# Four attention batches and two feed-forward layers on one core: part of the second layer's weights is rebuilt as float32 during attention

## The chip, the core and the metric

The kernel runs on one core of a Trainium2 chip. The metric is device microseconds of one execution. Engines are called PE (TensorE, with PEld for its weight loads), DVE (VectorE), ACT (ScalarE), POOL (GpSimd) and SP (SyncE, whose queue issues every DMA here).

## The reference, cut to what is computed

Causal attention with a forget gate over 4 batches, 8 heads, 576 positions of 64; its output, 2304 tokens of 512, goes through a first layer (512 to 1024, softmax gate, layer norm, back to 512) and a second (512 to 2048, square of Relu, back to 512).

```python
scores = scale * np.matmul(q, k.transpose(0, 1, 3, 2))
cum = np.cumsum(np.log(np.clip(f, 0.0001, 1.0)), axis=-1)
scores = np.where(causal, -1e9, scores + cum[:, :, :, None] - cum[:, :, None, :])
attn = np.exp(scores - np.max(scores, axis=-1, keepdims=True))
x = np.matmul(attn / (np.sum(attn, axis=-1, keepdims=True) + 1e-09), v)   # then tokens x 512
h = x @ w_in                                                              # 512 -> 1024
solu = h * softmax(h)
ln = (solu - mean(solu)) / np.sqrt(var(solu) + 1e-06) * g_ln
x = ln @ w_out                                                            # 1024 -> 512
h = np.maximum(x @ w2_in, 0.0)                                            # 512 -> 2048
out = h * h @ w2_out                                                      # 2048 -> 512
```

The weights w_in, w_out, w2_in and w2_out arrive as 64-bit floats, everything else as float32.

## The kernel before

**Split products.** A float32 matrix product is made of three products of a faster 32-bit type (fp32r): each operand is split into a rounded high part and the remainder, and high x low, low x high and high x high are added up in PSUM.

**Weights.** Each 64-bit weight is rebuilt as float32 in SBUF from its two 32-bit words by `convert` (L623): a DMA brings the words of 256 columns (256 KB) into a raw buffer (L629), ACT takes the high word (L643), one of ACT, DVE and POOL scales the low word down (through the helper `copy`, L303 to L311), DVE shifts (L647) and puts the sign in (L651), POOL adds the low word (L657). Then `copy` rounds the result to the high part and POOL or DVE subtracts to get the low part (L661). The first layer's weights are converted during the first 115 us (`weights1`). The second layer's weights are cut into 16 blocks of 128 hidden columns, four pieces each, 64 conversions (`weights2`). Their high and low parts go where attention and the first layer leave room: in order, the key buffers K1 and K2, spare ends of these, the first layer's weights and its small buffers. Six raw buffers (the transposed weights `pt`, `adj`, `x` of attention) are used in turn.

**Attention.** 20 tiles of up to 128 queries, 8 heads each. `load_k` and `load_q` bring a tile's keys and queries, in two halves of 4 heads (j = 0, 1); the host has laid out each half twice, on partitions 0 to 63 and 64 to 127, so that high and low part can be made in place. `prep_k` and `prep_q` split them (L421, L456); `picks` (L405) writes constant rows that pick each head's gate sums. For each head: PE makes scores in PSUM (L488), DVE adds the mask and takes the minimum of the negated scores (L509), ACT the exponent (L523), PE transposes (L543), ACT or DVE copies (L303) and, for two heads at a time, PE multiplies by the values (L564). At the end of a tile of tokens, `first` (L786 to L788 and a chain over DVE, ACT and POOL) and `out1` (L727 to L729) apply the first layer; `out1` stores the result split into `x2d` in DRAM.

**Second layer.** Six blocks of 384 tokens, 16 steps each (`step`, L1043). A step is an up product (12 matmuls, L1059 to L1061), Relu (L1067) and square (L1069) on ACT, rounding (L1070) and remainder (L1073) on DVE, and a down product (9 matmuls, L1089 to L1091). Blocks 0 and 1 are run side by side while the weights are converted; blocks 2 to 5 follow with all weights in place.

**Order.** Every operation is a step of a plan. `Plan.lay` (L97) is a list scheduler: it keeps a table of assumed times, takes for every engine the step that can start first (a lower priority number wins a tie), and emits instructions in that order. It may choose among ACT, DVE and POOL for copies and subtractions. Engines and SP's queue then run in that fixed order, each waiting where an operand is not there.

Of the kernel before, what the change touches and what calls it, by code (L numbers as in the profile page):

```python
# [11 lines left out]
U32 = mybir.dt.uint32  # L12
# [15 lines left out]
class Plan:  # L28
# [14 lines left out]
        dma=dict(pe=1000, dve=950, act=910, pool=950, dma=1290),  # L43
# [53 lines left out]
    def lay(self, slack=60):  # L97
# [52 lines left out]
        while todo:  # L150
            pick = None
            for e in engs:
# [23 lines left out]
                if e != "pe":  # L176
# [37 lines left out]
def tile_kernel(ctx: ExitStack, tc: tile.TileContext, q, k, v, f, w_in, w_out, g_ln, w2_in, w2_out, out):  # L214
# [29 lines left out]
    x2d = dram.tile([2, P, KC, NT], F32, name="x2d")  # L244
    sb = ctx.enter_context(tc.tile_pool(name="sb", bufs=1))
# [22 lines left out]
    QN = [new(f"qn{i}", [DM]) for i in range(2)]  # L268
# [116 lines left out]

    def load_q(n, prio):
        load("qn", QN, q, n, prio + 1)

    def load_v(n, prio):
# [7 lines left out]
        pl.add(dict(dma=800), fn, max(prio + 4, V0), writes=[("vn", n % NV)])  # L397

    def picks(i, j):
# [7 lines left out]
        s = pl.add(dict(dve=602, pool=1252) if i else dict(dve=602), fn, -6.9e6 if i == 0 else 5000, ["ident"], [("qa", i, j)], port=True)  # L407

    def prep_k(n, prio):
# [5 lines left out]
        for j in range(2):  # L415
# [7 lines left out]
            def auxrows(y, j=j):  # L423
# [9 lines left out]
                dict(dve=67 + 1.045 * HH * m, pool=119 + 2.213 * HH * m), lo, prio + 2 * j, [("kn", j)] + hk, lk,  # L433
# [9 lines left out]
    def prep_q(n, prio):  # L443
        m = tiles[n]["m"]
        i = n % 2
        for j in range(2):
            q1, q2 = Q1[i][j], Q2[i][j]
            raw = QN[j][:, 0 : HH * m].rearrange("p (h s) -> p h s", s=m)
            for rows, dst, nm in ((LO, q2, "qh"), (HI, q1, "qd")):
                copy(  # L450
                    HH * m, lambda rows=rows, dst=dst: dst[rows, :, 0:m], lambda rows=rows, raw=raw: raw[rows],
                    prio + 2 * j, [("qn", j)], [(nm, i, j)], (), SC, False,
                )

            def lo(q1=q1, q2=q2, raw=raw):
                nc.vector.scalar_tensor_tensor(  # L456
                    out=q1[LO, :, 0:m], in0=raw[LO], scalar=SC, in1=q2[LO, :, 0:m].bitcast(F32), op0=ALU.mult,
# [883 lines left out]
```

## Time and profile before

| | us |
|---|---|
| median of 3 runs | 898.15 |
| lowest, highest | 897.89, 899.88 |
| the profiled execution's own time | 895.01 |
| its span, first to last instruction | 892.9 |

The profile is of one execution. Its page gives for the whole span: PE busy 841.4 us (94%), PEld 728.5 (82%), DVE 459.4 (51%), ACT 496.5 (56%), POOL 294.1 (33%). These are averages over parts that differ; a table of busy times by stretch tells the parts apart. "Idle before" names how long an engine stood before an instruction and the engine and line that released it. The granted clock is TensorE's, 1.00 being 2.4 GHz.

### The profile page before, as it was taken

What the parts mean: (1) busy time and instruction counts of PE and PEld (TensorE: products, weight loads), DVE (VectorE), ACT (ScalarE), POOL (GpSimd) and SP (SyncE); (2) the same over time, 40 slices, a digit from 0 to 9 for tenths busy, and PEclk for the clock granted to TensorE, in tenths of its full rate; (3) what the DMA queues carried; (4) which work ended last, traced back from release to release, by engine and by line L of the source; (5) the groups of instructions that cost most, each with busy time, mean ns of one, the idle gap of its engine ahead of it and who ended that gap; (6) DMA issues with size and microseconds to landing.
All of it is one profiled execution on the core that took longest, in us unless ns stands there. A gap on an engine that the chain in (4) does not pass through costs nothing.

```text
span 892.9 us, 15185 instructions
## 1 busy us (share of the span) xinstructions
PE 841.4 (94%) x5360; PEld 728.5 (82%) x5360; DVE 459.4 (51%) x1139; ACT 496.5 (56%) x1286; POOL 294.1 (33%) x379
## 2 busy tenths in 40 slices
PE   3788899999999999999996999999999999999998
PEld 2556777888888888888875988899999999999997
DVE  6878666655655556655676789722222222222221
ACT  6889878666866667756675777523322222222222
POOL 6567756223521236211387788700000000000000
PEclk9979999999999999999998999999999999999999
DMA  6723335222511125010544644105002002000000
GB/s 219 233 86 126 106 108 157 83 59 66 171 48 37 59 67 165 29 42 24 162 145 132 223 140 131 48 1 177 36 0 72 36 1 71 36 1 1 36 0 36
DMA packets 55499, 75.26 MB, mean 84 GB/s; under 512 B 7456, under 2 KB 35104, under 8 KB 55424
## 3 DMA queue, kind: packets, MB, share of 16 engines
q1 hardware_dynamic: 55424, 74.30, 26.6%
q8 instruction: 42, 0.69, 0.3%
q14 instruction: 33, 0.27, 0.1%
HBM read 59.91 MB, written 14.30 MB: 83 GB/s over the span
## 4 chain that ended last, share of the span: by engine, by line
PE 77%; DVE 9%; DMA 5%; ACT 5%; issue 3%; POOL 2%; SPq 0%; POOLq 0%; DVEq 0%; ACTq 0%
PE pp L1059 6%; PE pp L1061 6%; PE pp L1060 6%; PE z L488 6%; PE pp L543 6%; PE xo L564 6%; PE pp L727 3%; PE hp L786 3%; PE hp L787 3%; PE hp L788 3%; PE pp L728 3%; PE pp L729 3%; PE hp L1089 2%; PE hp L1090 2%; PE hp L1091 2%
## 5 line engine op out<-in xcount | busy, mean ns | idle before, releaser
L1067 ACT ACTIVATE q<-pp 128x384 f32<-128x384 f32 x96 | 47.1, 491 | 223.1 <-PE pp L1061 221.0
L1070 DVE CAST q<-q 128x384 fp32r<-128x384 f32 x96 | 42.1, 438 | 243.4 <-PE xo L1091 92.3
L523 ACT ACTIVATE adj<-z,st 64x288 f32<-64x288 f32 (+9 forms) x192 | 94.9, 497 | 31.0 <-DVE st L509 29.3
L488 PE MATMUL z<-k,q 128*128 128x256 f32 (+17 forms) x384 | 95.1, 347 | 12.7 <-DVE q L456 9.1
L509 DVE CUSTOM_DVE_ANT_0 z<-z,maskb 128x128 f32<-128x128 f32 (+8 forms) x144 | 65.6, 464 | 52.8 <-PE z L488 49.9
L303 ACT COPY pt<-pp 128x384 f32<-128x384 f32 (+5 forms) x170 | 67.9, 420 | 39.0 <-PE pp L543 37.3
L543 PE MATMUL pp<-ident,adj 128*128 128x128 f32 (+1 forms) x480 | 78.7, 280 | 8.7 <-ACT adj L523 8.4
L727 PE MATMUL pp<-ln,woh 128*128 128x256 f32 x288 | 84.2, 292 | 2.3 <-ACT pt L303 2.3
L728 PE MATMUL pp<-ln,wol 128*128 128x256 f32 x288 | 80.8, 280 | 0.0
L729 PE MATMUL pp<-ln,woh 128*128 128x256 f32 x288 | 80.7, 280 | 0.0
L543 PEld LDWEIGHTS pp<-ident,adj 128*128 128x128 f32 (+1 forms) x480 | 52.8, 143 | 30.2 <-ACT adj L523 19.4
L488 PEld LDWEIGHTS z<-k,q 128*128 128x128 f32 (+3 forms) x384 | 58.4, 188 | 19.7 <-ACT q L305 7.9
L564 PE MATMUL xo<-pt,vn 128*64 128x128 f32 (+1 forms) x960 | 70.3, 278 | 3.8 <-ACT pt L303 3.1
L564 PEld LDWEIGHTS xo<-pt,vn 128*64 128x64 f32 x960 | 50.6, 140 | 23.6 <-issue 11.8
L786 PE MATMUL hp<-wih,xl 128*128 128x512 f32 x144 | 61.5, 427 | 2.2 <-ACT hp L825 1.8
L727 PEld LDWEIGHTS pp<-ln,woh 128*128 128x128 f32 x288 | 55.1, 191 | 5.3 <-ACT pt L303 2.6
L787 PE MATMUL hp<-wil,xh 128*128 128x512 f32 x144 | 57.2, 397 | 0.5 <-POOL wil L661 0.5
L788 PE MATMUL hp<-wih,xh 128*128 128x512 f32 x144 | 57.2, 397 | 0.0
L728 PEld LDWEIGHTS pp<-ln,wol 128*128 128x128 f32 x288 | 55.0, 191 | 0.5
L729 PEld LDWEIGHTS pp<-ln,woh 128*128 128x128 f32 x288 | 54.8, 190 | 0.0
L1069 ACT ACTIVATE q<-q 128x384 f32<-128x384 f32 x96 | 50.4, 525 | 2.5
L307 POOL TENSOR_SCALAR q<-qn 64x512 fp32r<-64x512 f32 (+1 forms) x43 | 28.0, 652 | 55.3 <-PE z L488 50.0
(470 smaller groups left out, 2233.5 us busy)
## 6 DMA issues: line engine op xcount, KB each, us to landing
x2d<-xc SPq DMA_DIRECT2D x72, 128.0 KB
kn<-in_k_dram SPq DMA_DIRECT2D x32, 256.0 KB
qn<-in_q_dram SPq DMA_DIRECT2D x32, 256.0 KB
vn<-in_v_dram SPq DMA_DIRECT2D x20, 256.0 KB
ln<-x2d SPq DMA_DIRECT2D x24, 192.0 KB
out_dram<-pt SPq DMA_DIRECT2D x18, 256.0 KB
pt<-in_moe_w_in_dram SPq DMA_DIRECT2D x17, 256.0 KB
ln<-in_moe_w_in_dram SPq DMA_DIRECT2D x8, 512.0 KB
```

The costliest lines, as they stand in the source:

```text
L303: nc.scalar.copy(dst(), src())
L488: nc.tensor.matmul(dst, lhsT=ql[0:r, p, 0:m], rhs=rhs, start=(g == 0), stop=(g == 1))
L509: nc.vector.tensor_tensor_reduce(out=z, in0=z, in1=maskb[0:m, o : o + e - a], scale=1.0, scalar=st[0:m, 0:1] if y else 3e38, op0=ALU.add, ...
L523: nc.scalar.activation(out=adj[0:m, c[1] : c[2]], in_=Z[c[0]][0:m, 0 : c[2] - c[1]], func=AF.Exp, bias=st[0:m, low : low + 1], scale=-1.0, ...
L543: nc.tensor.transpose(at(sk)[:, (c - g) * m : (c - g + 1) * m], adj[0:m, zc : zc + P], ident[0:m, 0:m])
L564: nc.tensor.matmul(XO[own[j], p, off : off + m], lhsT=VN[vslot[b, c]][:, (2 * p + j) * D : (2 * p + j + 1) * D], rhs=pts[j][:, c * m : (c ...
L727: nc.tensor.matmul(px, lhsT=woh[:, fc, w], rhs=lo, start=(fc == 0), stop=False)
L728: nc.tensor.matmul(px, lhsT=wol[:, fc, w], rhs=hi, start=False, stop=False)
L729: nc.tensor.matmul(px, lhsT=woh[:, fc, w], rhs=hi, start=False, stop=(fc == KF - 1))
L786: nc.tensor.matmul(HP[:, c], lhsT=XL[i][:, cc, :], rhs=wih[:, cc, w], start=(cc == 0), stop=False)
L787: nc.tensor.matmul(HP[:, c], lhsT=XH[i][:, cc, :], rhs=wil[:, cc, w], start=False, stop=False)
L788: nc.tensor.matmul(HP[:, c], lhsT=XH[i][:, cc, :], rhs=wih[:, cc, w], start=False, stop=(cc == KC - 1))
```

## The change

Four things are changed; the arithmetic of the results is not.

- Of 10 of the 16 blocks of the second layer's weights (`EARLY`), the first five operations of `convert` run earlier: `early2` adds 40 conversions with priorities from 140000 in steps of 7000, through one raw buffer (`ws`) and three result buffers (`ws`, and `q3` in the place that a second query buffer had). Each result is stored as float32 to a scratch tensor `w2d` in DRAM (128 KB). `again2` loads them back, 512 columns at a time (256 KB), into the six raw buffers and splits them: one rounding copy, one subtraction. The other 6 blocks go through `weights2` as before.
- The queries are laid out once by the host and loaded once for each tile, into one buffer `qn`; `prep_q` reads its two partition halves.
- The picking rows of the first tile have a priority before the gate's scan, those of the second one later (14000 for 5000); the subtraction for the first tile's keys may no longer go to POOL; the second part of the clip and scan has a later priority.
- The planner assumes longer DMA times, and leaves POOL unoccupied where a more urgent DVE operation that uses the port shared with POOL would become ready before POOL's ends.

```diff
-        dma=dict(pe=1000, dve=950, act=910, pool=950, dma=1290),
+        dma=dict(pe=1500, dve=1450, act=1410, pool=1450, dma=1790),
...
+                if e == "pool":
+                    end = c[0] + c[1].eng[e]
+                    x = [
+                        max(free["dve"], y.rdy["dve"]) for y in avail["dve"]
+                        if y.port and len(y.eng) == 1 and y.eng["dve"] and y.prio < c[1].prio - DUE
+                    ]
+                    if any(y < end and end - y > (y - c[0]) * WORTH for y in x):
+                        continue
...
+    w2d = dram.tile([EARLY, 2, P, 512], F32, name="w2d")
...
-    QN = [new(f"qn{i}", [DM]) for i in range(2)]
+    QN = new("qn", [DM])
...
     def load_q(n, prio):
-        load("qn", QN, q, n, prio + 1)
+        T = tiles[n]
+        m, o = T["m"], HH * T["q0"]
+        pl.add(
+            dict(dma=1140 * m / P), lambda: nc.sync.dma_start(QN[:, 0 : HH * m], q[T["b"], :, o : o + HH * m]), prio + 1,
+            writes=["qn"],
+        )
...
-        s = pl.add(dict(dve=602, pool=1252) if i else dict(dve=602), fn, -6.9e6 if i == 0 else 5000, ["ident"], [("qa", i, j)], port=True)
+        s = pl.add(dict(dve=602, pool=1252) if i else dict(dve=602), fn, -9.05e6 if i == 0 else 14000, ["ident"], [("qa", i, j)], port=True)
...
-                dict(dve=67 + 1.045 * HH * m, pool=119 + 2.213 * HH * m), lo, prio + 2 * j, [("kn", j)] + hk, lk,
+                dict(dve=67 + 1.045 * HH * m, pool=119 + 2.213 * HH * m) if n else dict(dve=67 + 1.045 * HH * m),
+                lo, prio + 2 * j, [("kn", j)] + hk, lk,
...
-    def convert(src, raw, w, hi, lo, n, prio, rawk, wk, outk, gain=None):
+    def convert(src, raw, w, hi, lo, n, prio, rawk, wk, outk, gain=None, to=None):
...
+        if to is not None:
+            pl.add(dict(dma=570), lambda: nc.sync.dma_start(to, w()), prio, [wk], [outk])
+            return
...
+    def early2():
+        q3 = {}
+        kw = [("wsw", 1), ("q3", 0), ("q3", 1)]
+        for n in range(4 * EARLY):
+            fc, g = divmod(n, 4)
+            c, hf = divmod(g, 2)
...
+            convert(
+                source2(fc, g), raw, w, None, None, 256, EARLY0 + n * EARLYP, ("wsr", 1), kw[n % 3],
+                ("w2d", fc, c, hf), to=w2d[fc, c, :, hf * 256 : hf * 256 + 256],
+            )
+
+    def again2(fc, prio):
...
+            def sub(raw=raw, hi=hi, lo=lo, c=c):
+                eng = nc.gpsimd if ls[c].on == "pool" else nc.vector
+                eng.tensor_tensor(out=lo(), in0=raw(), in1=hi().bitcast(F32), op=ALU.subtract)
+
+            pl.add(
+                dict(dma=1140), lambda raw=raw, c=c: nc.sync.dma_start(raw(), w2d[fc, c]), prio - AHEAD,
+                [("w2d", fc, c, z) for z in (0, 1)], rk,
+            )
+            copy(512, hi, raw, prio, rk, [("w2", fc, c, z, "h") for z in (0, 1)], (), None, False)
...
-        weights2(fc, TEND - 3000 + fc * W2P)
+        (again2 if fc < EARLY else weights2)(fc, TEND - 3000 + min(fc, EARLY) * W2E + max(fc - EARLY, 0) * W2P)
...
+EARLY, EARLY0, EARLYP = 10, 140000.0, 7000
+W2E = 2500
```

In the whole program, counts change so: 40 fewer raw-word loads in the transition and 40 more during attention, 40 stores to `w2d`, 20 loads from it, 20 instead of 40 query loads; PE's 4882 matmuls stay. What stands where is shown at three places. (Line numbers of the changed kernel are higher: L405 is L418 there, L421 is L434, L456 is L470, L509 is L526, L647, L651, L657, L661 are L665, L669, L675, L679; the subtraction of `again2` is L1008. Numbers behind a name count its buffers.)

DVE at the start, before: scan of the gate sums, split of the first queries (`q`), picking rows L405.

```order
L1158 TENSOR_SCALAR adj_30_97<-adj_30_97 32x448
L1151 SCALAR_TENSOR_TENSOR adj_32_99<-e_116,adj_31_98 32x128
L1170 CAST xh_45_112<-adj_32_99 32x128
L1173 TENSOR_TENSOR xh_45_112<-adj_32_99,xh_45_112 32x128
L1151 SCALAR_TENSOR_TENSOR adj_32_99<-e_116,adj_32_99,adj_31_98 32x448
L456 SCALAR_TENSOR_TENSOR q_12_79<-qn_22_89,q_16_83 64x512
L456 SCALAR_TENSOR_TENSOR q_13_80<-qn_23_90,q_17_84 64x512
L405 TENSOR_TENSOR q_16_83<-ident_67 16x512
L405 TENSOR_TENSOR q_17_84<-ident_67 16x512
L1183 TENSOR_TENSOR pt_51_174<-adj_32_99,pt_50_166 32x576
L509 ISA z_117,st_36_103<-z_117,maskb_68 128x128
```

The same place after:

```order
L418 TENSOR_TENSOR q_16_84<-ident_68 16x512
L418 TENSOR_TENSOR q_17_85<-ident_68 16x512
L1245 TENSOR_SCALAR adj_29_97<-adj_29_97 32x128
L1245 TENSOR_SCALAR adj_29_97<-adj_29_97 32x448
L1238 SCALAR_TENSOR_TENSOR adj_31_99<-e_116,adj_30_98 32x128
L1257 CAST xh_44_112<-adj_31_99 32x128
L1260 TENSOR_TENSOR xh_44_112<-adj_31_99,xh_44_112 32x128
L1238 SCALAR_TENSOR_TENSOR adj_31_99<-e_116,adj_31_99,adj_30_98 32x448
L434 TENSOR_TENSOR k_10_78<-kn_20_88,k_8_76 64x4x128
L470 SCALAR_TENSOR_TENSOR q_12_80<-qn_90,q_16_84 64x512
L434 TENSOR_TENSOR k_11_79<-kn_21_89,k_9_77 64x4x128
L470 SCALAR_TENSOR_TENSOR q_13_81<-qn_90,q_13_81 64x512
```

The picking rows moved ahead of the clip and the scan, and the two key subtractions came over from POOL, in between the splits of the queries; the first minimum (L526 there) still comes behind the query splits.

DVE in the middle of attention, in the tenth tile (two minima a head, of 288 columns each), before:

```order
L509 ISA z_117,st_37_104<-z_117,maskb_68 128x288
L509 ISA st_37_104 128x1
L509 ISA z_118,st_37_104<-z_118,maskb_68,st_37_104 128x288
L509 ISA st_37_104 128x1
L754 TENSOR_TENSOR xc_1103<-pp_121,xc_1103 128x128
```

The same place after:

```order
L526 ISA z_117,st_36_104<-z_117,maskb_69 128x288
L526 ISA st_36_104 128x1
L526 ISA z_118,st_36_104<-z_118,maskb_69,st_36_104 128x288
L526 ISA st_36_104 128x1
L665 TENSOR_SCALAR q_53_1517<-q_53_1517 128x256
L669 SCALAR_TENSOR_TENSOR q_53_1517<-ws_497,q_53_1517 128x256
L776 TENSOR_TENSOR xc_1142<-pp_121,xc_1142 128x128
```

The two DVE operations of an early conversion came in behind a head's minima.

POOL at the end of attention, where the second layer's first weights are made (`k` are the key buffers, now theirs), before:

```order
L307 TENSOR_SCALAR pt_54_4464<-pt_54_4464 128x256
L657 TENSOR_TENSOR adj_54_4476<-adj_54_4476,pt_54_4464 128x256
L307 TENSOR_SCALAR k_54_4503<-adj_54_4476 128x256
L661 TENSOR_TENSOR k_54_4503<-adj_54_4476,k_54_4503 128x256
L657 TENSOR_TENSOR adj_54_4476<-adj_54_4476,adj_54_4450 128x256
L661 TENSOR_TENSOR k_54_4551<-adj_54_4476,k_54_4551 128x256
L307 TENSOR_SCALAR pt_54_4549<-pt_54_4549 128x256
L307 TENSOR_SCALAR pt_54_4561<-pt_54_4561 128x256
```

The same place after:

```order
L675 TENSOR_TENSOR ws_497<-ws_497 128x256
L318 TENSOR_SCALAR k_54_4725<-pt_54_4700 128x512
L318 TENSOR_SCALAR ws_497<-ws_497 128x256
L675 TENSOR_TENSOR q_53_1517<-q_53_1517,ws_497 128x256
L615 TENSOR_TENSOR xl_47_115<-x_109,xh_45_113 128x512
L1008 TENSOR_TENSOR k_54_4790<-pt_54_4700,k_54_4790 128x512
L1008 TENSOR_TENSOR k_54_4725<-pt_54_4788,k_54_4725 128x512
L1008 TENSOR_TENSOR k_54_4779<-pt_54_4800,k_54_4779 128x512
L858 TENSOR_TENSOR sm_42_110<-sm_42_110,mhalf_71 128x1
```

The pairs of add and subtraction of 256 columns gave way to single subtractions of 512 columns, with the last of the early conversions (`ws`, `q_53`) still among them.

## Rows read from the trace of the kernel before

**Rows 1.** Stretches: length, then busy PE, PEld, DVE, ACT, POOL, clock, DMA, GB/s.
```profile
0.00:44.00 44.00, 24.51 (x118) 16.96 (x118) 32.50 (x72) 32.33 (x85) 25.87 (x36) 0.97 0.73 227
...
44.00:88.00 44.00, 36.36 (x215) 26.71 (x215) 36.55 (x83) 39.56 (x97) 30.79 (x35) 0.85 0.34 106
...
132.00:154.00 22.00, 21.12 (x175) 16.16 (x174) 14.95 (x59) 18.59 (x67) 15.38 (x19) 1.00 0.56 172
...
154.00:434.00 280.00, 280.00 (x2270) 240.35 (x2269) 165.96 (x500) 189.29 (x526) 79.95 (x107) 1.00 0.24 72
...
220.00:242.00 22.00, 22.00 (x177) 18.51 (x176) 14.14 (x48) 17.29 (x55) 12.67 (x16) 1.00 0.52 164
...
462.00:506.00 44.00, 34.65 (x215) 31.95 (x214) 31.28 (x68) 29.06 (x80) 34.63 (x45) 0.92 0.46 146
...
434.00:573.00 139.00, 123.95 (x692) 109.54 (x691) 110.58 (x205) 95.59 (x250) 109.76 (x139) 0.98 0.49 152
...
573.00:893.00 320.00, 316.20 (x1589) 286.65 (x1587) 71.42 (x153) 87.27 (x172) 3.89 (x5) 1.00 0.11 35
```
**Rows 2.** Who waited for whom on TensorE: us in total, times, longest.
```profile
PE z L1089 <- DVE kn L1073: 3.2, 3, 1.7
...
PE hp L1089 <- DVE qn L1073: 2.1, 4, 0.7
```
**Rows 3.** Order of time in the transition: start, us, engine, line, [idle before].
```profile
478.29 0.71 PE L1089 MATMUL z<-k,kn 128*128 128x512 f32 x1 [4.04 <-ACT adj L643]
...
474.04 0.43 ACT L305 ACTIVATE pt<-pt 128x256 uint32<-128x256 uint32 x1 [2.09 <-DMA pt<-in_moe_w_out_dram]
...
477.07 1.07 DVE L1073 TENSOR_TENSOR kn<-q,q 128x384 fp32r<-128x384 f32 x1
```
**Rows 4.** Groups of lines by shape, 434 to 573 us: xcount, busy, mean ns.
```profile
L657 POOL TENSOR_TENSOR adj<-adj,pt 128x256 uint32<-128x256 uint32 x22 | 18.2, 830 | 7.5 <-DVE adj L651 5.5 <-ACT x L303 1.3 <-ACT q L1069 0.7
...
L661 POOL TENSOR_TENSOR k<-adj,k 128x256 fp32r<-128x256 f32 x14 | 11.7, 834 | 5.1 <-ACT k L303 4.0 <-DMA pt<-in_moe_w_in_dram 1.0
...
L643 ACT ACTIVATE adj<-pt 128x256 f32<-128x256 f32 x21 | 9.0, 434 | 4.7 <-POOL wol L661 1.1 <-POOL woh L661 1.0 <-DMA pt<-in_moe_w_in_dram 0.9
```
**Rows 5.** The same view: 512-column subtractions and copies elsewhere.
```profile
L421 POOL TENSOR_TENSOR k<-kn,k 64x512 fp32r<-64x512 f32 x12 | 15.8, 1321 | 0.6
...
L421 DVE TENSOR_TENSOR k<-kn,k 64x512 fp32r<-64x512 f32 x3 | 2.1, 714 | 0.0
...
L303 ACT CAST k<-kn 128x512 fp32r<-128x512 f32 x5 | 2.9, 608 | 0.1
```
**Rows 6.** Two lines' own instructions, 434 to 573 us: duration ns min/median/max.
```profile
L647 DVE TENSOR_SCALAR adj<-adj x42: 279/296/844, 437.1 to 572.3; 128x256 uint32<-128x256 uint32 x42
...
L651 DVE SCALAR_TENSOR_TENSOR adj<-pt,adj x22: 411/426/965, 433.9 to 570.5; 128x256 uint32<-128x256 uint32 x22
```
**Rows 7.** The chain of waits: DMA pieces, start and us.
```profile
434.49 2.61 DMA adj<-in_moe_w_out_dram
...
437.31 4.25 DMA pt<-in_moe_w_in_dram
```
**Rows 8.** Order of time at the start, as in rows 3.
```profile
2.72 0.68 DVE L1158 TENSOR_SCALAR adj<-adj 32x128 f32<-32x128 f32 x2 [1.87 <-DMA adj<-in_f_dram]
...
8.45 3.10 DVE L405 TENSOR_TENSOR q<-ident 16x512 fp32r<-16x512 f32 x2
...
12.26 0.28 DVE L509 CUSTOM_DVE_ANT_0 z<-z,maskb 128x128 f32<-128x128 f32 x1
...
12.87 0.68 DVE L405 TENSOR_TENSOR q<-ident 16x512 fp32r<-16x512 f32 x1
...
10.21 0.98 PE L488 MATMUL z<-k,q 80*128 80x256 f32 x3 [1.68 <-DVE q L405]
...
21.19 0.66 ACT L643 ACTIVATE ln<-ln 128x512 f32<-128x512 f32 x1 [2.56 <-DMA ln<-in_moe_w_in_dram]
```

More of the change, by code (lines that the diff above doesn't have):

```diff
@@ L395, in fn @@
             nc.sync.dma_start(VN[n % NV], v[b, t * P : t * P + P])
-        pl.add(dict(dma=800), fn, max(prio + 4, V0), writes=[("vn", n % NV)])
+        pl.add(dict(dma=1140), fn, max(prio + 4, V0), writes=[("vn", n % NV)])
     def picks(i, j):
@@ L445, in prep_q, with lo @@
         i = n % 2
[L446 removed]
+        raw = QN[:, 0 : HH * m].rearrange("p (h s) -> p h s", s=m)
+        for j, src in enumerate(own):
             q1, q2 = Q1[i][j], Q2[i][j]
[L448 removed]
             for rows, dst, nm in ((LO, q2, "qh"), (HI, q1, "qd")):
                 copy(
[L451 to L452 removed]
+                    HH * m, lambda rows=rows, dst=dst: dst[rows, :, 0:m], lambda src=src: raw[src], prio + 2 * j, ["qn"],
+                    [(nm, i, j)], (), SC, False,
                 )
[L455 removed]
+            def lo(src=src, q1=q1, hi=(q1 if j else q2)):
                 nc.vector.scalar_tensor_tensor(
[L457 removed]
+                    out=q1[LO, :, 0:m], in0=raw[src], scalar=SC, in1=hi[src, :, 0:m].bitcast(F32), op0=ALU.mult,
                     op1=ALU.subtract,
                 )
[L461 removed]
+            pl.add(
+                dict(dve=67 + 1.045 * HH * m), lo, prio + 2 * j, ["qn", ("qd" if j else "qh", i, j)], [("ql", i, j)],
+                port=True,
+            )
     def head(s):
@@ L637, in convert @@
         lk, hk = rawk + ("l",), rawk + ("h",)
-        pl.add(dict(dma=max(350, 2.844 * n)), words, prio - AHEAD, writes=[lk, hk])
+        pl.add(dict(dma=4.45 * n), words, prio - AHEAD, writes=[lk, hk])
         def a1():
@@ L711, in weights1 @@
             )
+        return ws
     def out1(blk, ccs, prio, dp):
@@ L768, in out1 @@
                 wk = [("x2d", a, cc, 2 * blk + r) for r in range(2)]
-                pl.add(dict(dma=365), store(a), prio, [(nm, i, r) for r in range(2)], wk)
+                pl.add(dict(dma=570), store(a), prio, [(nm, i, r) for r in range(2)], wk)
     def first(x):
@@ new lines, in again2, with raw @@
+    def again2(fc, prio):
+        pieces = places[fc]
+        W2[fc] = [p[0] for p in pieces]
+        for c in range(2):
+            n = 2 * fc + c
+            ri = n % NRAW
+            rk = [("2r", ri, z) for z in "lh"]
+            if n < NRAW:
+                pl.add(dict(dve=0), lambda: None, prio, [], raws[ri][1] + rk)
+            for y, a in ((2 * c, "h"), (2 * c + 1, "l")):
+                pl.add(dict(dve=0), lambda: None, prio, [], list(pieces[y][1]) + [("w2", fc, c, z, a) for z in (0, 1)])
+            def raw(ri=ri):
+                tag = raws[ri][0]
+                if ("raw", tag) not in memo2:
+                    memo2["raw", tag] = new(tag, [512])
+                return memo2["raw", tag]
+            hi, lo = pieces[2 * c][0], pieces[2 * c + 1][0]
+            def sub(raw=raw, hi=hi, lo=lo, c=c):
+                eng = nc.gpsimd if ls[c].on == "pool" else nc.vector
+                eng.tensor_tensor(out=lo(), in0=raw(), in1=hi().bitcast(F32), op=ALU.subtract)
+            pl.add(
+                dict(dma=1140), lambda raw=raw, c=c: nc.sync.dma_start(raw(), w2d[fc, c]), prio - AHEAD,
+                [("w2d", fc, c, z) for z in (0, 1)], rk,
+            )
+            copy(512, hi, raw, prio, rk, [("w2", fc, c, z, "h") for z in (0, 1)], (), None, False)
+            if c == 0:
+                ls = {}
+            ls[c] = pl.add(
+                dict(pool=1252, dve=602), sub, prio, rk + [("w2", fc, c, z, "h") for z in (0, 1)],
+                [("w2", fc, c, z, "l") for z in (0, 1)], port=True,
+            )
@@ L1226, in tile_kernel @@
     load_v(1, LOAD1)
-    weights1(PIN0, POUT0)
+    early = weights1(PIN0, POUT0)
+    early2()
     for n in range(NQ):
```

54 lines of the change are left out of this document (31 added, 23 removed).

## The prediction

> **What bounds the kernel now.** I read three views in turn: busy times by stretch, what TensorE waited for, and the order of time where it waited. By stretch [rows 1] there are four regimes. Up to 154 us the vector engines set the pace: from 44 to 88 us ScalarE is busy 39.56 of 44 us. From 154 to 434 us TensorE has no idle time, while ScalarE works 189.29, VectorE 165.96 and GpSimd 79.95 of 280 us. From 573 us on TensorE is full again (316.20 of 320). Between them, from 434 to 573 us, TensorE is busy 123.95 of 139 us: 15.1 us idle, 9.4 of it in the 44 us from 462 to 506. There the granted clock is 0.92, a mix of its levels 1.2 and 2.4 GHz, with the longest idle times around it; 0.08 x 34.65 busy us is another 2.8 us. So this transition can give back 17.9 us at most.
>
> TensorE waits there by name for VectorE's split L1073, 3.2 + 2.1 us [rows 2], and longest in the row at 478.29 us, 4.04 us [rows 3]. The rows before it show the pattern. ScalarE, in order, stood 2.09 us until 474.04 for a conversion's DMA; the square and the rounding behind it were late, and the split of the step ran from 477.07 to 478.14, beside a GpSimd add. TensorE had nothing else, because the next step's weights were not converted either. GpSimd is the pace of that: it is busy 109.76 of the 139 us [rows 1], 104 of them 63 adds L657 and 62 subtractions L661 at 0.83 us [rows 4].
>
> **The transition after the change.** 40 of the 64 conversions leave it. In their place stand 20 loads of ready float32, 20 rounding copies of 512 columns and 20 subtractions; in the new order GpSimd has 8 of the subtractions, VectorE 12. GpSimd: 24 x 1.66 + 8 x 1.32 [rows 4, 5], the 6 us of other work, and some 4 us of late early conversions make 60 us instead of 109.76. ScalarE: 40 x 0.43 for L643 alone leave (17 us), about 17 x 0.61 = 10 come. VectorE: 40 x (0.30 + 0.43) = 29 leave at the median durations [rows 6], 12 x 0.71 = 9 come. None of the three is near the 121 us that TensorE needs (123.95 less the clock's 2.8), so TensorE becomes the bound. Its own order there is nearly the same, so the gain must come from waits that end earlier. Not all go: the chain Relu, square, cast, split between an up and a down product is not shortened, only less disturbed. I leave 4 us of the 17.9, most of the 5.3 named for the split, and take **-14 us**; bounds -7 (the 5.3 stay, and half of the rest) and -18 (nothing left).
>
> **The 40 conversions beside attention.** Each puts the first five operations there, without the two that split: ScalarE 0.43 (L643), a halfword scaling of the same width (in the order 8 on ScalarE, 32 on GpSimd), VectorE 0.30 + 0.43, GpSimd 0.83, a load of 256 KB and a store of 128 KB. To the 280 us ScalarE gets 48 x 0.43 = 21 and, in the order, 11 more query copies of some 0.6: 189.29 becomes 217, 78%. VectorE gets between 40 x 0.73 = 29 and, all beside GpSimd, 40 x (0.84 + 0.97) = 72 [rows 6]: 70 to 85%. GpSimd gets 40 x 0.83 + 32 x 0.5 = 49: 46%. From 220 to 242 us ScalarE was at 17.29 of 22 (79%) and TensorE lost nothing; from 132 to 154 at 18.59 (84%), and TensorE lost 0.88 of 22 [rows 1]. The new average is at the first, the densest tiles near the second. I take **+2 us**; bounds 0, and 280/22 x 0.88 = 11.
>
> The new store waits, on SP's queue, for GpSimd's add, and behind it stand the loads of keys, queries and values. They are issued about a tile (15 to 40 us) ahead, so nothing is on the path; without that lead each would cost its landing, 2.61 to 4.25 us [rows 7]. The DMA engines are busy 0.24 of this stretch at 72 GB/s; 40 x 384 KB less some 3 MB of queries add about 45 GB/s. All 40 pieces pass one raw buffer, one after the other: landing, then 0.43 + 0.30 + 0.43 + 0.83 and the hops between, 5 to 7 us a piece, 200 to 280 in all; from about 140 us that ends by 340 to 420. In SP's order the last stores stand among the first loads of ready pieces, and they are of the tenth weight block, which TensorE needs some 80 us later.
>
> **The start.** VectorE writes the picking rows L405 at 8.45 us, 3.10 us for two, beside GpSimd's key subtractions; TensorE's second score product waits for them until 10.21, and the first minimum runs at 12.26 [rows 8]. Alone the same instruction takes 0.68. After the change both come first, in VectorE's idle time before f lands (2.72); they end near 3.2 and push the scan by some 0.5 us. Behind the scan (now 6.7) stand four operations of 0.7, two of them GpSimd's key subtractions, and the 0.75 of L1183. The first head's operands are there after two, at 8.1, and the minimum can run at 10.2: 2 us earlier. Next late is the load of the first layer's weights, for which ScalarE stood 2.56 us until 21.19. A tile now has one query load where it had two: until 27 us that is 2 x 256 KB less, 2.3 us at the 227 GB/s of this stretch. ScalarE is nearly full from there to 115 us, so an earlier start is kept and a shorter load only in part: **-3 us**, bounds 0 and -7 (2 + 2.3 + 2.56). The later second half of the scan, the planner's DMA costs and its holding back of GpSimd only move the order and have no price of their own; what hides them is the slack above, and if it is gone they are in the bound of 11.
>
> **Sum.** -14 + 2 - 3 = -15. The profiled execution took 895.01 us (span 892.9 and 2.1 around it), so 880; the runs' median is 898.15, 3.1 above it. I forecast 898.15 - 15 = **883 us**.
>
> **A rule that speaks against it.** L647 takes 0.28 at least and 0.84 at most, L651 0.41 and 0.97 [rows 6]: up to 0.56 is added, two thirds of a GpSimd add. The Trainium skill, SBUF — State Buffer, section "Who interferes with whom", says that VectorE and GpSimd share a port pair as an exclusive lock and that the loser blocks until the other's instruction is done. The trace agrees with it in these rows. By that rule 40 conversions carry 80 chances of a blocked VectorE into the stage where its minimum stands between score and exponent; rival 1 works that out.
>
> **Rivals.** (1) *Slower: a blocked VectorE holds up attention.* If both VectorE operations of a conversion run beside GpSimd they take 0.84 + 0.97 instead of 0.30 + 0.43, 1.1 us longer; the minimum queued behind, the exponent, the transposes and TensorE's in-order queue are late by it. 40 x 1.1 = 44 us against -17 elsewhere: 925 us. It decides from 17/40 = 0.43 us a conversion that reaches TensorE. For it: the medians above lie beside maxima two to three times as long. Against: GpSimd would be busy 46% here, against 79% in the stretch these come from, and TensorE lost nothing at 79% of ScalarE. 8%. (2) *The transition keeps half its waits*, on the chain from up to down product or on loads of ready weights: -7 + 2 - 2, 891 us. For it: the 5.3 us on L1073. 17%. (3) *Everything lands*: -18 + 0 - 5, 875 us. 12%. (4) *It does not do what it says*: pieces come so late through the one buffer that the last blocks are missing when TensorE asks; at 8.5 us a piece they would end at 480 us and give back some 8 of the 14: 891 us. Against: 5 to 7 us above. 5%. (5) *No change*: the loss beside attention eats the gain. 3%.
>
> **Chances.** Forecast (878 to 888) 55%, the rest as above. The range 872 to 893 holds the forecast and (2), (3) and (4) nearly whole; (1), (5) and their tails stay out. About 0.2% (1.8 us) is what a measurement of this kernel can tell from no change. Faster 0.89, same 0.03, slower 0.08.
>
> **What the next profile would show.** Right: TensorE idle below 6 us in the transition, its clock 1.00; GpSimd near 60 us there; no waits named for L643; the first minimum near 10 us; TensorE still without idle time from about 150 us to the end of attention. Wrong: TensorE waiting for exponent or minimum in that stretch (rival 1); more than 8 us on the split L1073 (rival 2); TensorE waiting for loads or copies of ready weights (rivals 2, 4).

## The result, and the profile after

The changed kernel takes 875.36 us (median of 4 runs, 874.10 to 876.41), against 898.23 for the kernel before (4 runs): a ratio of 0.9741, 95% interval 0.9724 to 0.9759. That is 22.9 us less, where 15 were forecast; the range of 872 to 893 holds it. The profiled execution took 874.10 us (span 872.0), 20.9 less than the profiled one of before.

To see where the time went, I took the start of the same TensorE instruction in both traces (each holds 5360 matmul records), counted within its line, at three marks: the 145th score product (L488; early in attention, with the first layer's weights converted), the last value product (L564; the end of attention) and the 73rd first down product (L1089; the end of the transition).

| | 145th score | last value product | 73rd down product |
|---|---|---|---|
| before, us | 170.51 | 436.76 | 591.55 |
| after, us | 165.42 | 433.24 | 570.49 |
| gain of the stage | 5.1 | -1.6 | 17.5 |

From the third mark to the end the two kernels take the same time within 0.23 us. By stretch, after (start and length in us, then busy PE, PEld, DVE, ACT, POOL, granted clock, DMA share, GB/s):

```profile
32.00:80.00 48.00, 37.98 (x237) 27.84 (x238) 43.10 (x93) 45.27 (x109) 33.83 (x39) 0.95 0.42 126
80.00:132.00 52.00, 51.29 (x423) 41.67 (x424) 38.56 (x106) 44.86 (x133) 35.17 (x51) 0.95 0.39 121
154.00:434.00 280.00, 279.27 (x2258) 238.34 (x2257) 189.78 (x565) 205.56 (x572) 118.28 (x166) 1.00 0.39 116
434.00:573.00 139.00, 136.88 (x768) 124.47 (x767) 74.55 (x153) 68.97 (x158) 63.00 (x75) 1.00 0.37 115
462.00:506.00 44.00, 42.44 (x257) 39.19 (x256) 26.42 (x64) 24.99 (x62) 24.11 (x32) 1.00 0.57 177
```

The last two rows answer to those of the same stretches in [rows 1]: GpSimd is busy 63.00 us where it had 109.76, TensorE stands 2.1 of 139 us where it stood 15.1, and from 462 to 506 its clock is 1.00 where it was 0.92. The third row shows where the conversions went: VectorE 190 us for 166, ScalarE 206 for 189, GpSimd 118 for 80, and TensorE still stands only 0.7 of 280 us.

What TensorE waited for from 434 to 573 us, after (who waits, for whom, us in total, times, longest), to be read against [rows 2]:

```profile
PE z L1176 <- DVE kn L1160: 1.6, 2, 1.3
PE hp L1176 <- DVE q L1160: 0.5, 1, 0.5
```

L1160 is the split L1073 of before. It is the only wait with a name that is left, 2.1 us of the 5.3.

Between the marks the stage itself, before and after, same columns (443 to 591 us of before does the work of 440 to 570 after):

```profile
443.00:591.00 148.00, 132.96 (x703) 117.77 (x703) 111.23 (x206) 94.61 (x246) 109.43 (x136) 0.98 0.41 130
```
```profile
440.00:570.00 130.00, 127.88 (x703) 116.04 (x702) 69.55 (x142) 64.39 (x150) 58.16 (x71) 1.00 0.36 113
```

For the same 703 matmul rows, 12.9 of the 18 us are idle time that is gone, and 5.1 are busy time, 2.7 of that by the clock (0.02 x 132.96). What made the other 2.4 is not shown.

### The profile page after: what moved, and what is told of

It is laid out like the page before. It is cut to its first block, busy times and chain, and to the rows that moved or that the text cites. A ratio compares the mean times of both kernels' runs of the same rounds, so it can differ in the third digit from the quotient of the medians.

```text
span 872.0 us, 15164 instructions
## 1 busy us (share of the span) xinstructions
PE 838.4 (96%) x5360; PEld 727.3 (83%) x5360; DVE 449.1 (52%) x1152; ACT 485.1 (56%) x1237; POOL 283.5 (33%) x375
## 4 chain that ended last, share of the span: by engine, by line
PE 85%; ACT 6%; DVE 4%; issue 2%; POOL 2%; DMA 1%; ACTq 0%; POOLq 0%; DVEq 0%
PE pp L1148 7%; PE pp L1147 7%; PE pp L1146 7%; PE pp L560 6%; PE xo L581 6%; PE z L505 6%; PE pp L749 4%; PE hp L808 4%; PE pp L750 3%; PE pp L751 3%; PE hp L810 3%; PE hp L809 3%; PE z L1176 2%; PE z L1178 2%; PE z L1177 2%
## 5 line engine op out<-in xcount | busy, mean ns | idle before, releaser
L1157 DVE CAST q<-q 128x384 fp32r<-128x384 f32 x96 | 38.7, 403 | 267.5 <-PE xo L1178 92.3
L560 PE MATMUL pp<-ident,adj 128*128 128x128 f32 (+1 forms) x480 | 80.5, 284 | 15.5 <-ACT adj L540 14.6
L314 ACT COPY pt<-pp 128x256 f32<-128x256 f32 (+5 forms) x170 | 68.8, 422 | 35.6 <-PE pp L560 33.2
L560 PEld LDWEIGHTS pp<-ident,adj 128*128 128x128 f32 (+1 forms) x480 | 54.7, 146 | 36.3 <-ACT adj L540 24.3
L526 DVE CUSTOM_DVE_ANT_0 z<-z,maskb 128x128 f32<-128x128 f32 (+8 forms) x144 | 65.8, 463 | 34.3 <-PE z L505 31.9
L540 ACT ACTIVATION_READ_ACCUMULATOR adj<-z,st 128x1 f32 (+1 forms) x192 | 37.8, 197 | 0.0
```

The lines of the kernel that those rows point to most:

```text
L314: nc.scalar.copy(dst(), src())
L526: nc.vector.tensor_tensor_reduce(out=z, in0=z, in1=maskb[0:m, o : o + e - a], scale=1.0, scalar=st[0:m, 0:1] if y else 3e38, op0=ALU.add, ...
L540: nc.scalar.activation(out=adj[0:m, c[1] : c[2]], in_=Z[c[0]][0:m, 0 : c[2] - c[1]], func=AF.Exp, bias=st[0:m, low : low + 1], scale=-1.0, ...
L560: nc.tensor.transpose(at(sk)[:, (c - g) * m : (c - g + 1) * m], adj[0:m, zc : zc + P], ident[0:m, 0:m])
```

## Experiments

Each ratio is taken against runs of the kernel before on the same chip as the experiment. The marks, as gains over the trace of the kernel before (positive is earlier), sort all of them by stage. Two kernels with the same order up to the end of attention (`early0` and `early0_noadd`) differ by 1.4 us at the first mark, and two profiles of one kernel (`startorder`, `startorder_again`) by 0.25; so a single difference below 1.5 us at the start says nothing. The medians of the kernel before lie between 895.2 and 898.2 us beside the different rows, so medians of different rows can be compared to within some 3 us only.

| kernel | median us | ratio, 95% | start | attention | transition |
|---|---|---|---|---|---|
| changed | 875.4 | 0.9741 (0.9724 to 0.9759) | 5.1 | -1.6 | 17.5 |
| early0 | 887.6 | 0.9896 (0.9871 to 0.9920) | 5.5 | -0.8 | 4.2 |
| early0_noadd | 880.5 | 0.9823 (0.9779 to 0.9867) | 4.1 | -0.8 | 11.8 |
| early5 | 877.1 | 0.9782 (0.9731 to 0.9832) | 4.8 | -2.9 | 16.4 |
| nobeside | 875.0 | 0.9757 (0.9734 to 0.9779) | 4.5 | -2.2 | 18.0 |
| early0_oldplan | 893.7 | 0.9963 (0.9940 to 0.9986) | -0.5 | -1.1 | 1.1 |
| olddma | 883.3 | 0.9867 (0.9836 to 0.9899) | 4.2 | -3.6 | 13.6 |
| nohold | 875.6 | 0.9782 (0.9754 to 0.9809) | 3.7 | -3.1 | 18.3 |
| qtwice | 884.5 | 0.9875 (0.9843 to 0.9907) | -0.5 | -6.3 | 17.4 |
| early0_qspare | 888.2 | 0.9910 (0.9879 to 0.9941) | 3.3 | -0.8 | 4.2 |
| latepicks | 879.8 | 0.9831 (0.9803 to 0.9858) | -0.3 | -2.3 | 16.8 |
| startorder | 872.4 | 0.9728 (0.9695 to 0.9760) | 8.1 | -1.0 | 17.9 |
| startorder_again | 871.0 | 0.9741 (0.9715 to 0.9766) | 8.4 | -1.1 | 17.8 |

### What the early conversions are worth

**early0** takes them back and keeps the rest.

```diff
...
-EARLY, EARLY0, EARLYP = 10, 140000.0, 7000
+EARLY, EARLY0, EARLYP = 0, 140000.0, 7000
```

> The changed kernel with EARLY = 0: all 64 conversions of the second layer's weights stand in the transition again, everything else of the change is kept (picking rows, query loads, planner costs). Theory (the transition's 18 us come from the conversions that left it, the start's 5 us from the other edits, attention's loss of 2 us from the early conversions): 875.4 + 18 - 2 = 891 us (889 to 894); TensorE idle again by some 15 us between the end of attention and the full stretch, GpSimd near 110 us busy there. Rival (the other edits, above all the planner's DMA costs, made part of the transition's gain): 883 us or below, with TensorE idle under 8 us in the transition.

Measured: 887.6 us, between the two. The start's gain stays whole (5.5 us), and the transition gains 4.2 us over before without one early conversion. So the early conversions are worth 12.2 us, not all that the transition gained. The stretch of the transition and TensorE's waits in it:

```profile
443.00:591.00 148.00, 137.64 (x719) 120.90 (x718) 109.39 (x195) 93.65 (x245) 107.37 (x133) 0.98 0.41 125
```
```profile
PE z L1176 <- DVE kn L1160: 3.9, 4, 1.4
PE hp L1176 <- DVE qn L1160: 2.3, 4, 1.1
PE pp L1146 <- ACT k L314: 1.9, 2, 1.1
PE pp L1147 <- POOL k L679: 1.8, 3, 0.7
```

GpSimd is as busy as before, and TensorE waits for the split, for the rounding L314 and for GpSimd's subtraction L679. What is gone are the waits for ScalarE's L643; in the kernel before they are the longest from 434 to 591 us:

```profile
PE z L1089 <- ACT xw L643: 4.1, 2, 3.6
PE z L1089 <- ACT adj L643: 4.0, 1, 4.0
```

ScalarE itself stood 7.9 us there before loads that had not landed, and 0.6 in early0.

**early0_noadd** tests whether GpSimd is the pace: the same order, with its 64 adds of the transition left out.

```diff
-        pl.add(dict(pool=tt), a5, prio, [lk], [wk])
+        pl.add(dict(pool=tt), a5 if rawk[0] != '2r' else lambda: None, prio, [lk], [wk])
```

> The kernel with EARLY = 0 (887.6 us) in its own order, with GpSimd's 64 adds of the transition left out (the second layer's weights are other numbers; the 64 subtractions and all of ScalarE's and VectorE's operations stay). GpSimd's busy time there falls from 107 to some 55 us. Theory (GpSimd is the pace of the transition, and the early conversions gained by unloading it): the 12 us come back, 875.6 us (874 to 878), TensorE's waits for the split L1160 and for L314 gone. Rival (the chain on ScalarE and VectorE sets it, since they keep 64 conversions each): at most 4 us, 884 us or more, with the waits for the split still there.

Measured: 880.5 us; the transition gains 11.8 us over before, against 4.2 and 17.5.

```profile
443.00:585.00 142.00, 135.11 (x727) 121.14 (x726) 89.06 (x196) 89.47 (x245) 58.33 (x73) 1.00 0.42 131
```
```profile
PE z L1176 <- DVE kn L1160: 4.0, 4, 2.3
PE pp L1146 <- ACT k L314: 1.6, 3, 0.8
PE pp L1147 <- POOL k L679: 1.2, 3, 0.4
```

GpSimd's load is as low as after the change (58.33 us) and 7.6 of the 13.3 us come back, 2.8 of them as clock (0.02 x 137.64). The other 5.7 do not: the split's 4.0 us and the rounding's 1.6 stay, as the rival expected, while the split's second row falls from 2.3 to 0.2. Both are right in part. GpSimd's adds make more than half of the loss; that the queues of VectorE and ScalarE make the rest is what the named waits suggest, and no run took it apart. VectorE's busy time also fell by 20 us, with no VectorE operation left out: its operations no longer run beside GpSimd's adds. So the run does not tell GpSimd's own queue from what its adds cost VectorE.

**early5** takes 20 conversions early instead of 40.

```diff
-EARLY, EARLY0, EARLYP = 10, 140000.0, 7000
+EARLY, EARLY0, EARLYP = 5, 140000.0, 7000
```

> The changed kernel with EARLY = 5: 20 conversions beside attention, 44 in the transition; GpSimd would be busy some 82 us there (109.8 less 20 x 1.66, and 4 x 1.3 more). Theory (every GpSimd microsecond taken out gives its share, 0.3 us a conversion): 887.6 - 6 = 881.6 us. Rival (a threshold: it is enough that GpSimd falls below the 121 us that TensorE needs with some margin): 876 us, as with ten. A third (the first five blocks matter little, since TensorE's waits stand later): 885 or more.

Measured: 877.1 us. The transition gains 16.4 us, so the first 20 conversions bring 12.2 us and the next 20 another 1.1.

```profile
444.00:580.00 136.00, 132.89 (x717) 119.21 (x716) 88.59 (x167) 79.34 (x203) 77.12 (x99) 1.00 0.38 118
```
```profile
PE hp L1176 <- DVE qn L1160: 1.9, 2, 1.1
PE z L1176 <- DVE kn L1160: 1.0, 2, 0.8
```

The gain levels off, as the rival expected: with GpSimd busy 57% of the stage instead of 73%, the clock stays at its higher level and no weights are waited for. Whether there is a sharp threshold, and where between 0 and 20 conversions, no run shows.

### What they cost beside attention

**nobeside** runs the changed kernel in its own order with the early conversions left out, loads and stores among them.

```diff
+    cut = len(pl.steps)
     early2()
+    for s in pl.steps[cut:]:
+        s.fn = lambda: None
...
-nc.sync.dma_start(raw(), w2d[fc, c])
+nc.sync.dma_start(raw(), q[0, :, 0:512])
```

> The changed kernel in its own order on every engine, with the 40 early conversions left out (no loads, no operations, no stores; the 20 later loads take query words instead of the converted ones, so the second layer's weights are other numbers). Theory (the early conversions cost attention 2 us by loading the vector engines): 873.4 us, with the loss between 165 and 440 us gone. Rival 1 (they cost nothing, attention's 2 us are due to another order of its work): 875.4 us. Rival 2 (they cost more, hidden by gains of the new order): below 871 us.

Measured: 875.0 us. Attention is no faster without them: it loses 2.2 us against before, with them 1.6. That is rival 1: the conversions themselves cost nothing that can be measured. That the loss belongs to the order in which attention's own operations now stand is what is left, and not shown by a run of its own. How often GpSimd holds VectorE up can be read in the changed kernel, from 150 to 434 us (count, busy us, mean ns, idle before):

```profile
L669 DVE SCALAR_TENSOR_TENSOR q<-ws,q 128x256 uint32<-128x256 uint32 x25 | 11.4, 454 | 0.5
L665 DVE TENSOR_SCALAR q<-q 128x256 uint32<-128x256 uint32 x24 | 8.0, 334 | 9.6 <-ACT q L661 9.6
L669 DVE SCALAR_TENSOR_TENSOR ws<-ws 128x256 uint32<-128x256 uint32 x12 | 5.5, 457 | 0.3
L665 DVE TENSOR_SCALAR ws<-ws 128x256 uint32<-128x256 uint32 x12 | 3.7, 308 | 1.7 <-ACT ws L661 1.6
```

The means are 0.03 to 0.06 us above the least of [rows 6] (0.28 and 0.41). A conversion loses about 0.1 us of VectorE's time to GpSimd, where rival 1 needed 0.43 us to reach TensorE.

### What the planner's numbers are worth

**early0_oldplan** puts the old DMA costs back and drops the holding back of GpSimd, with no early conversions.

```diff
-        dma=dict(pe=1500, dve=1450, act=1410, pool=1450, dma=1790),
+        dma=dict(pe=1000, dve=950, act=910, pool=950, dma=1290),
...
-        pl.add(dict(dma=4.45 * n), words, prio - AHEAD, writes=[lk, hk])
+        pl.add(dict(dma=max(350, 2.844 * n)), words, prio - AHEAD, writes=[lk, hk])
...
-                if e == "pool":
+                if e == "none":
```

> The kernel with EARLY = 0 (887.6 us) with the planner's DMA costs back at their old numbers and its holding back of GpSimd left out; the start's other edits stay. Theory (these two edits gave the 4 us that the transition gained without any early conversion): 891.6 us, with the transition's loss back at that of before. Rival 1 (the 4 us are due to the order that the start left, not to the costs): 887.6. Rival 2 (these edits also made the start's gain): 896.

Measured: 893.7 us, between the theory and its second rival. The transition's extra gain is nearly gone (1.1 us for 4.2), as the theory had it: ScalarE stands 9.6 us there before loads that have not landed, and TensorE 5.0 us for L661, which is L643 of before. The start's gain is gone too (-0.5 for 5.5), as the rival had it, although the picking rows and the single query load are still there. The marks overstate this somewhat, since the profiled execution (895.2 us) is the longest of ten (890.3 to 895.2).

**olddma** and **nohold** undo one of the two each, in the changed kernel. The diff of olddma is the first two hunks above, with the costs of the other loads and stores put back likewise (cut there); that of nohold is the last.

> The changed kernel (875.4 us) with the planner's DMA costs alone back at their old numbers; holding back, picking rows, one query load and the early conversions stay. Theory (the costs gave the start's 5 to 6 us: with the old ones ScalarE stands in its fixed order before operations whose loads have not landed): 880.9 us (879 to 883), ScalarE waiting 5 us or more for DMAs before 132 us, against 0 in the changed kernel. Rival (it is the holding back of GpSimd): 875.4 us, with no such waits.

> The changed kernel (875.4 us) without the planner's holding back of GpSimd; its DMA costs and everything else stay. Theory (the DMA costs made the start's gain): 875.4 us, within 2 us either way, no waits of ScalarE for DMAs before 132 us. Rival (GpSimd's operations take the shared stretches from VectorE at the start, and holding them back made the gain): 880 us or more, with VectorE's busy time before 132 us longer by several us for the same operations.

Measured: 883.3 and 875.6 us. The old costs lose 7.9 us, but not where I put them: at the start 0.9 us (within the uncertainty), in attention 2.0, in the transition 4.0, against 3.1 without early conversions. Leaving out the holding back loses 0.2 us in the median and 2.2 by the marks; by the ratio it is 0.4% behind, with intervals that overlap. How long ScalarE stood for DMAs until 132 us, in the kernel before, the changed one, olddma and early0_oldplan:

```profile
ACT ln L643 <- DMA ln<-in_moe_w_in_dram: 3.5, 2, 2.6
ACT ws L643 <- DMA ws<-in_moe_w_out_dram: 2.7, 2, 2.0
```
```profile
ACT ws L661 <- DMA ws<-in_moe_w_out_dram: 0.2, 1, 0.2
```
```profile
ACT k L314 <- DMA kn<-in_k_dram: 2.5, 2, 1.7
ACT xc L661 <- DMA xc<-in_moe_w_out_dram: 0.9, 1, 0.9
```
```profile
ACT k L314 <- DMA kn<-in_k_dram: 6.9, 2, 5.2
ACT xc L661 <- DMA xc<-in_moe_w_out_dram: 0.8, 1, 0.8
```

With the old costs ScalarE stands in its fixed order before loads that have not landed, 3.4 to 7.7 us; with the longer ones 0.2 (0.9 in startorder). The theory expected 5 us or more for olddma; its 3.4 us cost the start less than one by the first mark, but 3.5 us of TensorE's idle time, which the next section counts.

### What the start is made of

**qtwice** issues each query load twice into the same buffer, **early0_qspare** (on early0) the second time into a spare one. Both keep the order of their base.

```diff
-            dict(dma=1140 * m / P), lambda: nc.sync.dma_start(QN[:, 0 : HH * m], ...), prio + 1,
+            dict(dma=1140 * m / P), lambda: [nc.sync.dma_start(QN[:, 0 : HH * m], ...) for y in range(2)], prio + 1,
```
```diff
+            dict(dma=1140 * m / P), lambda: [nc.sync.dma_start(y[:, 0 : HH * m], ...) for y in (QN, QX)], prio + 1,
```

> The changed kernel in its own order, with each query load issued twice in a row into the same buffer, so that the queries take the traffic they took before. Theory (3 of the start's 5 us come from the shorter query loads; before, ScalarE stood 2.6 and 2.7 us at the start for weight loads and after the change for none): 878.4 us, with TensorE late by 2 to 4 us already at 60 us. Rival (the start's gain is the new order of the first operations): 875.4 us (875 to 876).

> The kernel with EARLY = 0 (887.6 us) in its own order, with each query load issued a second time into a spare buffer: the traffic of before, but no waiting of the second load for the landing of the first, which the earlier run with one buffer had. Theory (the traffic and the places in SyncE's queue cost by themselves): +4 us, 891.6, nearly all of it before 60 us. Rival 1 (the earlier 9 us were the queue standing for a landing): 887.6. Rival 2 (the traffic costs all of it): 896.

Measured: 884.5 us, 9.2 more, and 888.2, 0.7 more than its base. The first is no measure of the traffic. Its second load waits on SyncE's queue for the landing of the first, and all later loads stand behind it; the queue's own waits from 0 to 165 us:

```profile
SPq L398 <- DMA qn<-in_q_dram: 26.7, 10, 6.6
```

That was rival 1 of early0_qspare. With a spare buffer the same traffic costs 0.7 us in the median and 2.2 at the first mark, of which 1.4 is what two equal orders differ by. Of the 2.3 us that I gave the shorter load, 1 may be real; the runs cannot tell it from none.

**startorder** undoes two of the three edits of the start's order, **latepicks** the picking rows alone. The later second part of the clip and scan stays in every run.

```diff
-        s = pl.add(..., fn, -9.05e6 if i == 0 else 14000, ["ident"], [("qa", i, j)], port=True)
+        s = pl.add(..., fn, -6.9e6 if i == 0 else 5000, ["ident"], [("qa", i, j)], port=True)
...
-                dict(dve=67 + 1.045 * HH * m, pool=119 + 2.213 * HH * m) if n else dict(dve=67 + 1.045 * HH * m),
+                dict(dve=67 + 1.045 * HH * m, pool=119 + 2.213 * HH * m),
```

> The changed kernel with the picking rows back behind the first splits and the first key subtractions free to go to GpSimd, as before the change. Theory (2 us of the start's 5 come from here; ScalarE's first exponent would be 1 us later): 877.4 us, the first minimum past 12 us. Rival 1 (the start's gain is all in the query loads): 875.4 us. Rival 2 (all of it is here): 880.4 us.

> The changed kernel (875.4 us) with the picking rows alone back behind the first splits; the first key subtractions stay on VectorE. In the run with both undone the time was 872.4 us. Theory (the early picking rows bring nothing that is kept; the order that follows from them decides within some 3 us): 872 to 876 us, the first minimum later than in the changed kernel. Rival (they bring the 2 us forecast): 877.4 us.

> The kernel with the picking rows and the first key subtractions as before the change, which took 872.4 us (870.1 to 874.9), against 875.4 for the changed kernel. Theory (it is faster by some 3 us, all of it won before 165 us, since VectorE's work meets less of GpSimd's there): 872.4 us, ratio to the kernel before 0.971 to 0.974. Rival (chance of a single build on one chip): 875 us, ratio 0.974 to 0.976.

Measured: 872.4, 879.8 and 871.0 us. The two differ by 8.4 us at the first mark, in opposite directions from the changed kernel, though one holds the other's edit. No expectation of startorder and latepicks fits: putting the picking rows late costs 5.4 us at the start if the key subtractions stay on VectorE and, with these freed too, 3 are won. Up to the first mark every kernel runs the same 951 to 955 matmul rows, so the time up to it can be split into TensorE's busy and idle time. Before, changed, startorder, latepicks, olddma and early0_oldplan, each until its own mark:

```profile
0.00:170.51 170.51, 137.72 (x955) 106.45 (x955) 121.87 (x313) 136.62 (x373) 105.09 (x136) 0.94 0.46 143
0.00:165.42 165.42, 138.25 (x954) 107.62 (x955) 127.20 (x318) 138.20 (x373) 109.34 (x144) 0.94 0.45 138
0.00:162.39 162.39, 134.68 (x955) 103.77 (x955) 127.98 (x326) 135.26 (x363) 105.38 (x145) 0.96 0.46 141
0.00:170.80 170.80, 141.56 (x954) 109.08 (x955) 127.27 (x322) 141.97 (x383) 102.08 (x135) 0.93 0.44 136
0.00:166.30 166.30, 135.66 (x951) 105.55 (x952) 129.35 (x330) 139.84 (x377) 96.99 (x133) 0.95 0.46 142
0.00:170.95 170.95, 139.36 (x954) 109.64 (x955) 128.52 (x320) 133.09 (x359) 102.42 (x142) 0.93 0.42 127
```

The idle time is 32.8, 27.2, 27.7, 29.2, 30.6 and 31.6 us. Kernels of one order differ in it by less than 1 us (startorder_again 26.9; early0 and early0_noadd 27.8 and 28.0), and nohold has 27.3. So startorder does not wait less than the changed kernel: its 3.0 us are busy time, at a granted clock of 0.96 for 0.94. Of latepicks' 5.4 us, 2.1 are idle and 3.3 busy time, at 0.93. With the old DMA costs 3.5 (olddma) and 3.7 us (early0_oldplan against early0) of idle time come back; olddma's start is only 0.9 us later because TensorE was also busy 2.6 us less, at 0.95. Busy time at a lower clock can stand where a wait would have stood, so the two parts are not independent, and this stays a reading.

The single executions of startorder's two builds bear it out. Seven with a granted clock of 0.990 or 0.992 over the whole span took 870.1 to 872.4 us, three with 0.987 or 0.988 took 873.9 to 874.9; the changed kernel's four, at 0.986 to 0.988, took 874.1 to 876.4. At the same clock the two kernels are within some 1 us of each other. For latepicks this does not hold (878.8 to 880.8 us at 0.985 to 0.990): its loss is not the clock alone, and what the rest is stays open.

startorder_again repeats the time that its theory expected, but not for the reason given there, less meeting of VectorE and GpSimd: VectorE is busy 127.98 us up to the mark, 127.20 in the changed kernel. By its medians startorder is 3 to 4 us shorter than the changed kernel. By the ratios to the kernel before the two cannot be told apart (0.9728 and 0.9741 against 0.9741).

## Why the prediction was right, and where its terms were off

The time fell on rival 3 (875 us, given 12%), inside the range but below the forecast's own 878 to 888. Its parts, -18, 0 and -5, are nearer to the measured -17.5, +1.6 and -5.1 than the forecast's -14, +2 and -3.

**The transition (-14, measured -17.5).** The mechanism was right: 40 conversions leave, GpSimd falls to 63 us where 60 were forecast, TensorE becomes the bound, its idle time is 2.1 us (below 6 forecast), its clock 1.00. The mis-sized step is "I leave 4 us of the 17.9": 2.1 of them stayed, since the split's waits fell from 5.3 to 2.1 us, and TensorE was busy some 2 us less than the clock accounts for, which no term had. Rival 2, which kept them, was too careful; half of what the 5.3 leave is 6.3, so its -7 was not quite its own sum. But the term mixed two causes. Some 3 to 4 us came from the planner's DMA costs (early0 without conversions 4.2, of which early0_oldplan keeps 1.1; olddma 13.6 for 17.5), which I had said have no price of their own; the conversions gave 13.3. Their price stood in the trace of before: TensorE waited 8.1 us for L643, more than the 5.3 for the split, behind a ScalarE that stood before loads. The forecast saw 4.04 us of it, and ScalarE's 2.09 us for a load ahead of that, and laid both to GpSimd. And "GpSimd is the pace" covers 7.6 of the 13.3 by early0_noadd, not all.

**Beside attention (+2, measured +1.6).** The size was right by luck, since its cause was not. It was derived from ScalarE's share; ScalarE did 206 us there where I reckoned 217, and without the conversions the loss is the same. The bound of 11 and rival 1 were far off.

**The buffers.** I let the early pieces end by 340 to 420 us. Stores of converted pieces, changed kernel (duration in ns min/median/max, first and last start):

```profile
L688 SPq DMA_DIRECT2D w2d<-q x26: 319/446/711, 154.3 to 450.4; - x26
L688 SPq DMA_DIRECT2D w2d<-ws x14: 382/443/482, 134.8 to 463.8; - x14
```

The last stands at 463.8 us, 8.4 us a piece, which is rival 4's 8.5. Its price did not come: TensorE waits for no load or copy of ready weights. That the late pieces are those of the tenth block, needed last, is the forecast's own argument for it and fits, but no run tested it.

**The start (-3, measured -5.1).** Here the mechanism failed and the size came out near it. The first minimum was to run at 10.2 us, 2 us earlier:

```profile
1.83 1.38 DVE L418 TENSOR_TENSOR q<-ident 16x512 fp32r<-16x512 f32 x2 [0.98 <-POOL ident masks.py:199]
...
5.37 1.13 DVE L1238 TENSOR_TENSOR_SCAN adj<-e,adj,adj 32x448 f32<-32x448 f32 x1
...
6.43 1.03 DVE L434 TENSOR_TENSOR k<-kn,k 64x512 fp32r<-64x512 f32 x1
...
7.99 1.09 DVE L434 TENSOR_TENSOR k<-kn,k 64x512 fp32r<-64x512 f32 x1
...
9.00 1.03 POOL L418 TENSOR_TENSOR q<-ident 16x512 fp32r<-16x512 f32 x1
9.11 1.48 DVE L470 SCALAR_TENSOR_TENSOR q<-qn,q 64x512 fp32r<-64x512 f32 x1
...
11.29 0.28 DVE L526 CUSTOM_DVE_ANT_0 z<-z,maskb 128x128 f32<-128x128 f32 x1
```

The picking rows do take 1.38 us for two and end at 3.2, as forecast (3.10 us for two before, [rows 8]). The two key subtractions then take 1.03 and 1.09 us where 0.7 was reckoned, the second query split runs beside GpSimd and takes 1.48 us instead of 0.68, and the minimum comes at 11.29, 1 us earlier. The Trainium skill's rule (SBUF — State Buffer, section "Who interferes with whom") was weighed in the prediction for attention only; the row of the second split agrees with it, with 0.8 us added. Even that microsecond is not kept: the 25th score product starts at 31.83 us, before at 31.81. The gain grows after it, from 32 to 132 us, where the same rows of before read:

```profile
32.00:80.00 48.00, 39.67 (x238) 28.82 (x237) 38.87 (x85) 41.73 (x105) 33.12 (x37) 0.86 0.40 125
80.00:132.00 52.00, 43.98 (x342) 35.35 (x341) 34.80 (x92) 41.19 (x112) 33.10 (x47) 0.93 0.34 103
```

There the three vector engines are 4.2, 3.5 and 0.7 us busier after the change in the first stretch and 3.8, 3.7 and 2.1 in the second: the same work is packed closer, and TensorE is busy 5.6 us more by 132 us (7.3 more in the second stretch, 1.7 less in the first). Before, TensorE's idle time from 80 to 132 us (52 - 43.98 = 8.0 us) is nearly all named for ScalarE: copies L303, exponent L523 and L825; after, 0.7 us are left. So the step that failed is that the planner's edits "only move the order and have no price of their own". By TensorE's idle time up to the first mark, 5.6 us went (32.8 to 27.2), and 3.5 of them come back with the old DMA costs alone, 0.2 without the holding back and 0.5 in startorder; 2.1 come back in latepicks, which is above what equal orders differ by and has no explanation here. The shorter query load is worth some 1 us at most, where 2.3 were reckoned. The rest of what the kernels differ by at that mark is busy time; for startorder it goes with the granted clock, for the others only in part. Which of the waits each cost of a load sets stays open. That the term came out near its size is luck.

**Base.** The profiled execution of before stood 3.1 us below its median, that of after 1.3; that accounts for 2 of the 22.9 us, and the forecast had carried the 3.1 over.

## What to carry to other kernels

When work is moved off a stage, try half of the move first: here half gave nine tenths of the gain, since the waits for weights were gone once the busiest helper stood at 57% of the stage instead of 73%. Where a list scheduler fixes the order, its assumed DMA times are part of the kernel: times that are too short put an in-order engine in front of loads that have not landed. Where an early stage is packed by such a scheduler, split an effect of a few us at a mark into the bound engine's idle and busy time before giving it to an edit: two orders that differed by 3 us in the end had the same idle time, and the difference went with the granted clock.

## What was not expected of the hardware

- A second load into the same buffer cost 9.2 us in all by SyncE's queue standing for the first one's landing (26.7 us of queue time until 165 us); the same traffic into another buffer cost 0.7 us, within the uncertainty.
- In the changed kernel's attention, from 150 to 434 us, VectorE's shift and sign took up to 0.95 and 1.17 us for medians of 0.29 and 0.42 (ns min/median/max), yet the mean excess over 36 and 37 of them stayed at 0.06 us or less, with GpSimd busy 42% of that stage:

```profile
L665 DVE TENSOR_SCALAR q<-q x24: 279/292/951, 163.8 to 432.6; 128x256 uint32<-128x256 uint32 x24
...
L669 DVE SCALAR_TENSOR_TENSOR q<-ws,q x25: 374/424/1173, 152.6 to 433.0; 128x256 uint32<-128x256 uint32 x25
```
